# Linear attention with a routed feed-forward part: the order of the results' products, of the loads, and a second bank

## The chip, the cores and the metric

One core of one Trainium2 chip runs the kernel. The time is the device time of one execution in microseconds (us), taken over several runs. TensorE is named PE in the profile (PEld is its loading of weights), VectorE DVE, ScalarE ACT, GpSimd POOL, and SyncE, which issues most of the transfers, SP.

## The reference

The input has 4 batches, 8 heads, 768 steps and 48 values per head. First comes a linear attention with a decay for each key channel, then, for each batch, a feed-forward part for the 128 rows of 768 with the highest score.

```python
for t in range(S):
    kt, vt, rt, wt = (k[:, :, t], v[:, :, t], r[:, :, t], w[:, :, t])
    cur = np.einsum('bhd,bhe->bhde', u[None] * kt, vt)
    y[:, :, t] = np.einsum('bhd,bhde->bhe', rt, state + cur)
    state = wt[:, :, :, None] * state + np.einsum('bhd,bhe->bhde', kt, vt)
# x: y with the heads side by side, 4 x 768 x 384
scores = np.einsum('bsd,d->bs', x, w_gate)
for b in range(B):
    top_idx = np.argpartition(-scores[b], capacity)[:capacity]   # 128 rows
    xe = x[b, top_idx]
    ye = np.maximum(xe @ w1, 0.0) @ w2                           # 384 -> 1024 -> 384
    out[b, top_idx] = xe + sigmoid(scores[b, top_idx])[:, None] * ye
```

## The kernel before, in words

The steps are cut into chunks of 128: 6 chunks for each of 4 batches, 24 in all, with all 8 heads of a chunk worked on at once. Heads lie in pairs: the two heads of a pair take partitions 0 to 63 and 64 to 127 (48 of 64 used), and four pairs lie side by side in the free dimension. Everything is float32; only the ranking uses bfloat16.

For a chunk, `decays_t` (L202) transposes the decays w on TensorE; `scans` (L206) runs two running products over them on VectorE, from the right (L212) and from the left (L224). `scaled` (L239) transposes k and r and multiplies them by these products, which gives K and R (L243). `scores` (L259) multiplies K by R for each head (L264) and `masked` (L269) keeps what lies before the diagonal (`sc`, L273). `outputs_t` (L282) makes the transposed result in one PSUM bank, `ps_yt`: for each pair two products of the values with `sc` (L290, the "value products", over all 128 partitions and half of the columns) and, where the chunk is not the first of its batch, two products of the state carried in with R (L298, the "state products", each on one half of the partitions). `carry_products` (L323) and `carry` (L335) make the state for the next chunk. `rows_out` (L305) transposes the result back into the same bank (`ps_y`), adds the chunk's own-step part `vo` on VectorE (x, L309) and stores it; `row_scores` (L315) makes the rows' routing scores (L318).

The four inputs lie in rings of buffers: 4 each for r, k and w, 5 for v. `load(n)` (L120) issues w, k, r and v of chunk n on SP's queue, each as one transfer of 192 KB in runs of 192 bytes. Chunks 0 to 3 are loaded ahead of the loop, with u and w_gate between them. The two feed-forward matrices of 1.5 MB each come in one issue each (L141).

The order of all work is written out by hand. `turn(i)` (L528) does, in this order: scores, mask, carry and transposed K of chunk i, K of chunk i+1, the rows out of chunk i-1; one piece of the ranking and some pieces of the feed-forward part; R of chunk i+1, the decay transposes of chunk i+2, the results' products and the carry's products of chunk i, further pieces of the feed-forward part; the scans of chunk i+2, the own values of i+1, the row scores of i-1, one more piece of the ranking; and last the loads of chunk i+5. It runs for i from -2 to 24. Every engine keeps to the order in which it is given its instructions, and so does SP with its transfers.

The ranking (`mixture`, L353) of a batch begins two turns after the batch's last chunk and goes piece by piece into later turns: rank transposes (L361), comparisons on VectorE (L380), rank sums (L389), one-hot rows (L405), row numbers (L412, L418), a gather of the 128 rows (L427), their transposes (L436). The feed-forward part (`forward`, L464) follows: 8 hidden products in two groups of four, each group in the one PSUM bank "m" (`ps_h`, L471) and emptied by a ScalarE activation into `hid` (L476), then 8 output products (`ps_f`, L481) in the same bank, and `ye` (L487), which is scattered to the output (L490). For batch 3, and a good part of batch 2, this stands behind the loop. At the end a check of the range of the decays picks a general version, which is not run with these inputs.

Of the kernel before, what the change touches and what calls it, by code (L numbers as in the profile page):

```python
# [10 lines left out]
FP32 = mybir.dt.float32  # L11
# [7 lines left out]
L = 128  # L19
DP = 64  # L20
NBUF = 4
# [17 lines left out]
def kernel(  # L39
# [39 lines left out]
    nc = tc.nc  # L79
    PSUM = bass.MemoryType.PSUM  # L80

    B, H, S, D = r.shape
# [3 lines left out]
    NCH = S // L  # L86
    HP = H // 2
    NDC = C // L
    NFC = F // L
# [27 lines left out]
            if i < len(bufs):  # L117
                nc.any.memset(bufs[i][:, :, D:DP], value)

    def load(n):  # L120
        if n >= N:
            return
        b, ci = chunks[n]
        for bufs, x in ((w_bufs, w), (k_bufs, k), (r_bufs, r), (v_bufs, v)):
            nc.sync.dma_start(
                out=bufs[n % len(bufs)][:, :, 0:D],
                in_=x[b, :, ci * L:(ci + 1) * L, :].rearrange("h t d -> t h d"),
            )

    load(0)  # L130
    u_bc = consts.tile([L, H, D], FP32)
    nc.sync.dma_start(out=u_bc, in_=_rows(u, L))
    load(1)
    wg_bc = consts.tile([L, C], FP32)
    nc.sync.dma_start(out=wg_bc, in_=_rows(moe_w_gate, L))
    load(2)
    load(3)
    w1 = consts.tile([L, NDC, F], FP32)
    w2 = consts.tile([L, NFC, C], FP32)

    def load_weights():  # L141
        nc.sync.dma_start(out=w1, in_=moe_w1.rearrange("(n p) f -> p n f", p=L))
        nc.sync.dma_start(out=w2, in_=moe_w2.rearrange("(n p) c -> p n c", p=L))


    ident = consts.tile([L, L], FP32)
# [135 lines left out]
    def outputs_t(t):  # L282

        n = t["n"]
        vt = v_bufs[n % VBUF]
        old = state.get(n)
        ps = psY.tile([L, HP, L], FP32, tag="y", name="ps_yt")
        for j in range(HP):
            for par in (0, 1):
                nc.tensor.matmul(  # L290
                    ps[DP * par:DP * par + DP, j, :], vt[:, 2 * j + par, :],
                    t["sc"][:, par, j, :], start=True, stop=(old is None),
                )
            if old is None:
                continue
            for par in (0, 1):
                rows = slice(DP * par, DP * par + DP)
                nc.tensor.matmul(  # L298
                    ps[DP * par:DP * par + D, j, :], old[rows, j, :], t["R"][rows, j, :],
                    start=False, stop=True,  # L300
                )
        t["yt"] = lev.tile([L, HP, L], FP32, tag="yt", name="yt")
        nc.scalar.copy(out=t["yt"], in_=ps)  # L303
# [160 lines left out]
    def forward(b, n, rows, where, xe, xeT, gate):  # L464

        hid = mod.tile([L, NFC, L], FP32, name="hid")
        for f0 in range(0, NFC, 4):
            ps = psM.tile([L, 4, L], FP32, tag="m", name="ps_h")
            for q in range(4):
                for dc in range(NDC):  # L470
                    nc.tensor.matmul(  # L471
                        ps[:, q, :], w1[:, dc, (f0 + q) * L:(f0 + q + 1) * L],
                        xeT[:, dc, :], start=(dc == 0), stop=(dc == NDC - 1),
                    )
                if q == 3:
                    nc.scalar.activation(out=hid[:, f0:f0 + 4, :], in_=ps, func=AF.Relu)  # L476
                yield

        ps = psM.tile([L, C], FP32, tag="m", name="ps_f")
        for fc in range(NFC):  # L480
            nc.tensor.matmul(  # L481
                ps, hid[:, fc, :], w2[:, fc, :], start=(fc == 0), stop=(fc == NFC - 1)
            )
            if fc < NFC - 1:
                yield
        ye = mod.tile([L, C], FP32, name="ye", bufs=2)
        nc.vector.scalar_tensor_tensor(  # L487
            out=ye, in0=ps, scalar=gate, in1=xe, op0=ALU.mult, op1=ALU.add
        )
        nc.gpsimd.indirect_dma_start(  # L490
            out=rows, out_offset=where, in_=ye[0:n], in_offset=None,
            bounds_check=(b + 1) * S - 1, oob_is_err=False,
        )
        yield
# [5 lines left out]
    def step(f, n, *more):  # L500
        if 0 <= n < N:
            f(work.setdefault(n, dict(n=n)), *more)
# [25 lines left out]
    def turn(i):  # L528
        if i - 2 >= 0 and i - 2 < N and chunks[i - 2][1] == NCH - 1:
            b = chunks[i - 2][0]  # L530
            mixing.append(mixture(b))
        step(own_products, i + 1)
        step(scores, i)
        step(masked, i)
        step(carry, i - 1, work.get(i))
        step(scaled, i + 1, "K", k_bufs, "right")
        step(back, i)
        step(rows_out, i - 1)
        mix()
        fed(PIECES // 2)  # L540
        step(scaled, i + 1, "R", r_bufs, "left")
        step(decays_t, i + 2)
        step(outputs_t, i)
        step(carry_products, i)
        fed(PIECES - PIECES // 2)
        step(scans, i + 2)
        step(range_check, i + 2)
        step(own_values, i + 1)
        step(row_scores, i - 1)
        mix()  # L550
        load(i + 1 + NBUF)
        if i == 0:
            load_weights()

    with tc.manual_schedule():
        for i in range(-2, N + 1):
# [93 lines left out]
```

## Time and profile before

| | us |
|---|---|
| median of three runs | 272.96 |
| lowest, highest | 271.13, 276.75 |
| the profiled execution | 272.69 |
| its span, from the first to the last record | 270.9 |

The rows in the section below come from this one profiled execution. Times in them count from the start of its span. "x4" behind an operation is a number of records; one float32 product shows as two.

### The profile page before, as it was taken

The numbers are of one execution on the slowest core, as the hardware profiler recorded it, in microseconds if no ns is written. First come the engines' busy times: TensorE is split into PE (matmuls) and PEld (weight loads), VectorE is DVE, ScalarE is ACT, GpSimd is POOL, SyncE is SP. The second block draws the span as 40 slices with busy tenths as digits, with TensorE's granted clock in tenths as the row PEclk, the third lists the DMA queues.
The fourth block names the chain that finished last, engine by engine and source line by source line (L and its number), as shares of the span: only waits on it lengthen the run. The fifth ranks groups of instructions, "written<-read, shape, count | busy, mean of one in ns | idle before, by whom it ended". The sixth has DMA issues, their size and how long they took to land.

```text
span 270.9 us, 5843 instructions
## 1 busy us (share of the span) xinstructions
PE 230.1 (85%) x2290; PEld 169.9 (63%) x2290; DVE 211.8 (78%) x431; ACT 77.0 (28%) x201; POOL 98.9 (37%) x108
## 2 busy tenths in 40 slices
PE   3783999999798699795999899994999899989780
PEld 2572677776665467674688476584778566685740
DVE  6894478999999998999999999789889994373010
ACT  5450203333442121344323213233213301220100
POOL 3243405554433550844055326334236331102000
PEclk9998569999999858999999999999899999999997
DMA  9999999999996363488545635944000000201001
GB/s 129 180 176 166 162 285 327 179 191 205 193 173 115 67 114 87 92 171 119 111 76 109 127 75 96 171 108 72 31 30 2 29 31 23 68 29 29 31 0 42
DMA packets 109732, 29.96 MB, mean 111 GB/s; under 512 B 104576, under 2 KB 108928, under 8 KB 109696
## 3 DMA queue, kind: packets, MB, share of 16 engines
q1 hardware_dynamic: 109184, 27.93, 58.2%
q0 software_dynamic: 512, 1.57, 1.8%
q8 instruction: 20, 0.33, 0.6%
q14 instruction: 16, 0.13, 0.2%
HBM read 23.99 MB, written 5.51 MB: 109 GB/s over the span
## 4 chain that ended last, share of the span: by engine, by line
PE 44%; DVE 7%; ACT 4%; issue 1%; POOL 0%; ACTq 0%
PE ps_h L471 9%; PE ps_f L481 8%; PE ps_yt L290 6%; PE ps_yt L298 6%; PE ps_t L199 5%; PE ps_s L264 4%; PE ps_kv L330 2%; ACT kt L278 1%; ACT hid L476 1%; PE ps_w L199 1%; DVE left L224 1%; PE ps_e L361 1%; DVE right_buf L212 1%; DVE scr L444 1%; PE ps_y L199 1%
## 5 line engine op out<-in xcount | busy, mean ns | idle before, releaser
L255 POOL TENSOR_TENSOR vo<-v_buf,own 128x384 f32<-128x384 f32 x24 | 25.2, 1051 | 106.5 <-DVE own L253 102.4
L290 PE MATMUL ps_yt<-sc,v_buf 128*64 128x128 f32 x384 | 41.8, 309 | 4.0 <-DVE x L309 4.0
L303 ACT COPY yt<-ps_yt 128x512 f32<-128x512 f32 x24 | 14.1, 586 | 106.9 <-PE ps_yt L298 99.0
L273 DVE TENSOR_TENSOR sc<-ps_s,before_f 128x512 f32<-128x512 f32 x48 | 30.8, 682 | 12.4 <-PE ps_s L264 12.4
L298 PE MATMUL ps_yt<-R,state 64*48 64x128 f32 x320 | 35.7, 302 | 0.0
L290 PEld LDWEIGHTS ps_yt<-sc,v_buf 128*64 128x64 f32 x384 | 20.1, 141 | 21.2 <-issue 14.1
L212 DVE TENSOR_TENSOR_SCAN right_buf<-ps_w,from_right 128x511 f32<-128x511 f32 x24 | 29.0, 1210 | 5.3 <-PE ps_w L199 5.3
L248 POOL TENSOR_TENSOR rk<-r_buf,k_buf 128x384 f32<-128x384 f32 x24 | 30.9, 1289 | 4.0 <-DMA r_buf<-in_r_dram 4.0
L224 DVE TENSOR_TENSOR_SCAN left<-ps_w,from_left 128x511 f32<-128x511 f32 x24 | 30.7, 1280 | 0.9
L264 PE MATMUL ps_s<-R,K 48*128 48x128 f32 x384 | 30.6, 304 | 0.0
L264 PEld LDWEIGHTS ps_s<-R,K 48*128 48x128 f32 x384 | 25.7, 204 | 4.6 <-issue 2.3
L471 PE MATMUL ps_h<-xeT,w 128*128 128x128 f32 x192 | 25.5, 283 | 2.0 <-ACT hid L476 1.4
L380 DVE SCALAR_TENSOR_TENSOR ahead<-every,score,behind 128x768 bf16<-128x768 f32 (+5 forms) x24 | 27.0, 1165 | 0.1
L481 PE MATMUL ps_f<-w,hid 128*128 128x384 f32 x64 | 24.3, 506 | 2.2 <-ACT hid L476 2.2
L249 POOL TENSOR_TENSOR rk<-rk,u_bc 128x384 f32<-128x384 f32 x24 | 25.3, 1053 | 2.6 <-DMA u_bc<-in_u_dram 0.8
L199 PE MATMUL ps_w<-ident,w_buf 128*128 128x128 f32 x96 | 16.5, 301 | 10.1 <-DVE slots L162 4.2
L471 PEld LDWEIGHTS ps_h<-xeT,w 128*128 128x128 f32 x192 | 23.1, 195 | 3.0 <-ACT hid L476 1.8
L298 PEld LDWEIGHTS ps_yt<-R,state 64*48 64x48 f32 x320 | 14.0, 123 | 15.2 <-issue 14.8
L278 ACT COPY kt<-ps_t 128x512 f32<-128x512 f32 x24 | 14.0, 585 | 30.3 <-PE ps_t L199 30.1
L199 PE MATMUL ps_t<-ident,r_buf 128*128 128x128 f32 x96 | 16.5, 298 | 3.7 <-ACT kt L278 2.3
L243 DVE TENSOR_TENSOR R<-ps_t,left 128x512 f32<-128x512 f32 x24 | 16.4, 684 | 3.9 <-PE ps_t L199 2.0
L199 PEld LDWEIGHTS ps_w<-ident,w_buf 128*128 128x128 f32 x96 | 12.7, 157 | 10.7 <-issue 10.7
(89 smaller groups left out, 326.1 us busy)
## 6 DMA issues: line engine op xcount, KB each, us to landing
w_buf<-in_w_dram SPq DMA_DIRECT2D x25, 192.0 KB, 4.1
k_buf<-in_k_dram SPq DMA_DIRECT2D x25, 192.0 KB, 4.8
r_buf<-in_r_dram SPq DMA_DIRECT2D x25, 192.0 KB, 5.0
v_buf<-in_v_dram SPq DMA_DIRECT2D x25, 192.0 KB, 4.3
out_dram<-x SPq DMA_DIRECT2D x24, 192.0 KB, 2.1
w<-in_moe_w_dram SPq DMA_DIRECT2D x2, 1536.0 KB, 9.7
u_bc<-in_u_dram SPq DMA_DIRECT2D x1, 192.0 KB, 4.6
wg_bc<-in_moe_w_gate_dram SPq DMA_DIRECT2D x1, 192.0 KB, 5.2
```

Of the source, the lines that this page charges most:

```text
L199: nc.tensor.transpose(ps[:, j, :], src(j), ident)
L212: nc.vector.tensor_tensor_scan(out=flat[:, W - 2::-1], data0=wt[:, W - 1:0:-1], data1=from_right.rearrange("p j t -> p (j t)")[:, W - 2::- ...
L224: nc.vector.tensor_tensor_scan(out=left.rearrange("p j t -> p (j t)")[:, 1:W], data0=wt[:, 0:W - 1], data1=start.rearrange("p j t -> p (j ...
L248: nc.gpsimd.tensor_mul(rk, r_bufs[n % NBUF][:, :, 0:D], k_bufs[n % NBUF][:, :, 0:D])
L249: nc.gpsimd.tensor_mul(rk, rk, u_bc)
L264: nc.tensor.matmul(ps[:, par, j, :], t["K"][rows, j, :], t["R"][rows, j, :], start=True, stop=True,)
L273: nc.vector.tensor_mul(t["sc"][:, par], ps[:, par], _heads(before_f, HP))
L290: nc.tensor.matmul(ps[DP * par:DP * par + DP, j, :], vt[:, 2 * j + par, :], t["sc"][:, par, j, :], start=True, stop=(old is None),)
L298: nc.tensor.matmul(ps[DP * par:DP * par + D, j, :], old[rows, j, :], t["R"][rows, j, :], start=False, stop=True,)
L380: nc.vector.scalar_tensor_tensor(out=ahead[:, c, lo:S], in0=every[:, lo:S], scalar=score[:, b, c:c + 1], in1=behind[:, 0:S - lo], op0=ALU. ...
L471: nc.tensor.matmul(ps[:, q, :], w1[:, dc, (f0 + q) * L:(f0 + q + 1) * L], xeT[:, dc, :], start=(dc == 0), stop=(dc == NDC - 1),)
L481: nc.tensor.matmul(ps, hid[:, fc, :], w2[:, fc, :], start=(fc == 0), stop=(fc == NFC - 1))
```

## The change

It has four parts.

1. Results' products: all eight value products of a chunk are issued first, then all eight state products. The bank's start flag is set by the first pair's value products alone.
2. Loads: the loads of one step are v of chunk n-2, k and r of chunk n-1 and w of chunk n, ahead of the loop and in it; the loop's first turn issues none. The feed-forward matrices are cut into seven pieces (three of 512 KB, four of 384 KB), one issued at the end of each turn from turn 2 on.
3. In the last turn the row scores are made right after the rows out.
4. For the last batch the second group of four hidden products uses the results' bank ("y").

```diff
-    def load(n):
-        if n >= N:
-            return
-        b, ci = chunks[n]
-        for bufs, x in ((w_bufs, w), (k_bufs, k), (r_bufs, r), (v_bufs, v)):
+    def load(bufs, x, n):
+        if n < N:
+            b, ci = chunks[n]
             nc.sync.dma_start(
                 out=bufs[n % len(bufs)][:, :, 0:D],
                 in_=x[b, :, ci * L:(ci + 1) * L, :].rearrange("h t d -> t h d"),
             )
 
-    load(0)
+    def loads(n):
+
+        load(v_bufs, v, n - 2)
+        load(k_bufs, k, n - 1)
+        load(r_bufs, r, n - 1)
+        load(w_bufs, w, n)
+
+    load(w_bufs, w, 0)
+    load(k_bufs, k, 0)
+    load(r_bufs, r, 0)
+    load(w_bufs, w, 1)
     u_bc = consts.tile([L, H, D], FP32)
     nc.sync.dma_start(out=u_bc, in_=_rows(u, L))
-    load(1)
+    loads(2)
+    loads(3)
     wg_bc = consts.tile([L, C], FP32)
     nc.sync.dma_start(out=wg_bc, in_=_rows(moe_w_gate, L))
-    load(2)
-    load(3)
...
-    def load_weights():
-        nc.sync.dma_start(out=w1, in_=moe_w1.rearrange("(n p) f -> p n f", p=L))
-        nc.sync.dma_start(out=w2, in_=moe_w2.rearrange("(n p) c -> p n c", p=L))
+    weights = [
+        (w1[:, i, :], moe_w1[i * L:(i + 1) * L, :]) for i in range(NDC)
+    ] + [
+        (w2[:, i:i + 2, :], moe_w2[i * L:(i + 2) * L, :].rearrange("(n p) c -> p n c", p=L))
+        for i in range(0, NFC, 2)
+    ]
+
+    def load_weights(n):
+        while n > 0 and weights:
+            to, src = weights.pop(0)
+            nc.sync.dma_start(out=to, in_=src)
+            n -= 1
...
         for j in range(HP):
             for par in (0, 1):
                 nc.tensor.matmul(
                     ps[DP * par:DP * par + DP, j, :], vt[:, 2 * j + par, :],
-                    t["sc"][:, par, j, :], start=True, stop=(old is None),
-                )
-            if old is None:
-                continue
+                    t["sc"][:, par, j, :], start=(j == 0), stop=(old is None),
+                    skip_group_check=True,
+                )
+        for j in range(HP if old is not None else 0):
             for par in (0, 1):
                 rows = slice(DP * par, DP * par + DP)
                 nc.tensor.matmul(
                     ps[DP * par:DP * par + D, j, :], old[rows, j, :], t["R"][rows, j, :],
-                    start=False, stop=True,
+                    start=False, stop=True, skip_group_check=True,
                 )
...
-            ps = psM.tile([L, 4, L], FP32, tag="m", name="ps_h")
+
+            pool, tag = (psY, "y") if b == B - 1 and f0 % 8 == 4 else (psM, "m")
+            ps = pool.tile([L, 4, L], FP32, tag=tag, name="ps_h")
...
         step(rows_out, i - 1)
+        if i == N:
+            step(row_scores, i - 1)
         mix()
...
-        step(row_scores, i - 1)
+        if i < N:
+            step(row_scores, i - 1)
         mix()
-        load(i + 1 + NBUF)
-        if i == 0:
-            load_weights()
+        if i > -2:
+            loads(i + 5)
+        if i > 1:
+            load_weights(1 if NCH > 2 else 100)
```

## Rows read from the trace of the kernel before

**Rows 1.** The page: busy time of each engine, and VectorE's slices.

```profile
PE 230.1 (85%) x2290; PEld 169.9 (63%) x2290; DVE 211.8 (78%) x431; ACT 77.0 (28%) x201; POOL 98.9 (37%) x108
...
DVE  6894478999999998999999999789889994373010
```

**Rows 2.** Stretches: length, busy PE, PEld, DVE, ACT, POOL, granted clock, DMA share, GB/s.

```profile
17.66:32.26 14.60, 10.21 (x88) 6.47 (x85) 9.01 (x18) 3.25 (x10) 5.04 (x6) 0.74 1.26 165
32.26:42.06 9.80, 9.80 (x86) 7.71 (x84) 6.54 (x12) 2.15 (x6) 1.29 (x2) 0.69 1.15 280
42.06:63.58 21.52, 20.80 (x240) 14.84 (x236) 19.73 (x39) 7.25 (x21) 10.55 (x12) 1.00 1.11 221
98.97:108.64 9.67, 9.58 (x108) 7.53 (x106) 8.25 (x17) 2.16 (x7) 1.93 (x3) 0.79 0.40 88
205.68:216.15 10.47, 9.42 (x99) 6.85 (x98) 10.37 (x20) 2.63 (x7) 5.26 (x5) 1.00 0.05 19
```

**Rows 3.** Waits of VectorE for TensorE: us in total, times, longest.

```profile
DVE sc L273 <- PE ps_s L264: 12.4, 10, 4.1
...
DVE R L243 <- PE ps_t L199: 2.0, 5, 0.7
```

**Rows 4.** Transfers: GB/s in 40 slices; issues of w with KB and us to landing.

```profile
GB/s 129 180 176 166 162 285 327 179 191 205 193 173 115 67 114 87 92 171 119 111 76 109 127 75 96 171 108 72 31 30 2 29 31 23 68 29 29 31 0 42
...
w_buf<-in_w_dram SPq DMA_DIRECT2D x25, 192.0 KB, 4.1
```

**Rows 5.** SP's issues in order of time (start, us): both loads of chunk 3's w.

```profile
14.72 1.09 SPq L125 DMA_DIRECT2D w_buf<-in_w_dram  x1
...
20.15 1.38 SPq L125 DMA_DIRECT2D w_buf<-in_w_dram  x1
```

**Rows 6.** TensorE in order of time, 20 to 26 us.

```profile
20.52 0.66 PE L199 MATMUL ps_t<-ident,r_buf 128*128 128x128 f32 x4 [0.24 <-ACT kt L278]
25.34 1.09 PE L199 MATMUL ps_w<-ident,w_buf 128*128 128x128 f32 x4 [4.15 <-DMA w_buf<-in_w_dram]
```

**Rows 7.** The chain (start, us to the next), and TensorE in order of time.

```profile
114.05 0.37 PE ps_yt L290 x4
114.42 0.35 PE ps_yt L298 x4
...
116.94 1.09 PE ps_s L264 x16
```

```profile
67.47 1.09 PE L290 MATMUL ps_yt<-sc,v_buf 128*64 128x128 f32 x16
68.39 0.62 PE L330 MATMUL ps_kv<-v_buf,kt 128*64 128x48 f32 x16
```

**Rows 8.** VectorE in order of time: score masks of chunks 2, 5, 6 and 23.

```profile
34.39 1.29 DVE L273 TENSOR_TENSOR sc<-ps_s,before_f 128x512 f32<-128x512 f32 x2 [4.07 <-PE ps_s L264]
...
58.02 1.29 DVE L273 TENSOR_TENSOR sc<-ps_s,before_f 128x512 f32<-128x512 f32 x2 [0.39 <-PE ps_s L264]
...
64.92 1.28 DVE L273 TENSOR_TENSOR sc<-ps_s,before_f 128x512 f32<-128x512 f32 x2
...
226.98 1.29 DVE L273 TENSOR_TENSOR sc<-ps_s,before_f 128x512 f32<-128x512 f32 x2 [2.96 <-PE ps_s L264]
```

**Rows 9.** Behind the loop, in order of time: VectorE's ye, TensorE's waits.

```profile
234.94 0.62 DVE L487 SCALAR_TENSOR_TENSOR ye<-ps_f,gate,xe 128x384 f32<-128x384 f32 x1 [0.36 <-PE ps_f L481]
...
236.09 0.32 PE L361 MATMUL ps_e<-ident,score 128*128 128x128 f32 x1 [0.64 <-DVE score L318]
...
253.69 2.94 PE L471 MATMUL ps_h<-xeT,w 128*128 128x128 f32 x24 [0.75 <-ACT hid L476]
257.32 0.91 PE L481 MATMUL ps_f<-w,hid 128*128 128x384 f32 x2 [0.69 <-ACT hid L476]
```

**Rows 10.** TensorE in order of time at 93 us.

```profile
93.07 0.69 PE L290 MATMUL ps_yt<-sc,v_buf 128*64 128x128 f32 x4 [2.23 <-DVE x L309]
93.69 0.67 PE L298 MATMUL ps_yt<-R,state 64*48 64x128 f32 x4
```

## The prediction

> **What bounds the kernel now.** I read the busy line and the slices of the page first. TensorE shows 85% and VectorE 78% of the span, and VectorE's slices are at 9 for most of the loop [rows 1]: two engines share the bound, so time taken from one is worth only what the other leaves idle. The stretches cut at the start of each turn's score products say which of the two it is. The turn 205.68 to 216.15 holds 10.37 us of VectorE work in 10.47 us: VectorE sets it. The two turns from 17.66 to 42.06 hold 9.01 of 14.60 and 6.54 of 9.80, with a granted clock of 0.74 and 0.69: there VectorE starves, by 5.59 + 3.26 us. In the next three turns, 42.06 to 63.58, it idles 21.52 - 19.73 = 1.79 us [rows 2]. The waits say for whom: ten times for the score products, 12.4 us together, five times for the product behind R, 2.0 us [rows 3].
>
> Why does the second turn starve? Chunk 3's w is issued at 14.72 and again at 20.15, because the preload has chunks 0 to 3 and the first turn asks for chunk 3 once more; the list of transfers has 25 w loads for 24 chunks [rows 4, 5]. TensorE's transpose of that w waits for the second copy until 25.34, 4.15 us. After that gap the engine runs at its lower level, 1.2 GHz of 2.4, as the four transposes show that take 1.09 us there [rows 6], and the next scores reach VectorE 4.07 us late [rows 8].
>
> **Part 1, loads.** A load is 196,608 bytes; the slices from 7 to 34 us move 162 to 180 GB/s, 170 or so: 1.16 us per load [rows 4]. The second w of chunk 3 is the 19th in the queue and there at 25.34, so the nth is there near 3.3 + 1.16 n us. In the new order (w, k, r, w, u, then v, k, r, w twice) chunk 3's w is the 13th and is not repeated: 18.4 us. It is needed when the r transposes before it end, which start at 20.52 [rows 6]: near 21. Turn 2 needs k, r and w of the next chunk, 16th to 18th: 21.9 to 24.2, needed a turn of about 7 us later than in turn 1, near 26 to 28. Turn 3 needs the 20th to 22nd: 26.5 to 28.8, needed near 33. So no wait for a transfer is left, with 2.6 us to spare or more. The other bound is SP's issue spacing: from 14.72 to 20.15 it takes 5.43 us for four, 1.36 each [rows 5]. By it, and 4.1 us from issue to landing [rows 4], the 13th is there at 12 x 1.36 + 4.1 = 20.4 and the 18th at 27.2: just in time. I take 1.16, which comes from the bytes moved.
>
> With the 4.15 us gap gone the clock need not fall, and VectorE is late by nothing: from 58.02 to 64.92 one turn of its work takes 6.90 us [rows 8]. The idle time from 17.66 to 63.58 is 5.59 + 3.26 + 1.79 = 10.6 us. I take 10.2 of it; the last three turns need part 2 for theirs (about 1.2 us). The rest stays as the small steps between products and VectorE. The lower bound is 5: the wait goes, but the half clock comes anyway, from the wait for x that TensorE then has in the same place.
>
> The feed-forward weights, 3.1 MB in two issues at the end of turn 0, become seven pieces of 0.5 and 0.4 MB, issued after turns 2 to 8. Their first use is in batch 0's feed-forward part, four turns after the last piece. In these turns the queue carries four loads, one output row block (5 x 1.16 = 5.8 us) and a piece; at the 285 to 327 GB/s of the slices in which the weights went by [rows 4] a piece adds 1.2 to 1.8 us. That is 7.0 to 7.6 us against turns of 7 to 8: the transfers about keep up, and each load has one to two turns of lead. On SP each load still stands behind the output block of its turn, as before. Cost taken: 0, bounds 0 to 2 us.
>
> **Part 2, results' products in two runs.** In the chain of waits a pair of value products takes 0.37 us between starts and a pair of state products 0.35, alternating four times: 4 x 0.72 = 2.88 us. Eight value products alone, at a batch's first chunk, take 68.39 - 67.47 = 0.92 us, or 0.23 a pair; the score products, in the state products' form of half-height tiles, take 1.09 for eight including one change of form [rows 7]. So each change of form costs about 0.13 us, and there are eight. New: 0.92 + 1.09 + 0.14 = 2.15, a saving of 0.72 us in each of 20 turns, 14.5 us of TensorE time. Bounds: 0, if the changes are not what costs, to 1.0 in a turn at half clock.
>
> How much of it counts? In turns that VectorE sets, nothing. In the others it shortens the waits above. Of the 12.4 us, four waits before 60 us (first 4.07, last 0.39) are 5.5 and already in part 1; the last, at 226.98, is 2.96 [rows 3, 8]; five in the middle make 3.9. TensorE is late through several turns in a row there, so savings add up until VectorE is the late one. I take 3.6 of the 3.9 and 0.7 of the 2.0 us behind R: 4.3. At the loop's end two turns' savings are 1.44, of which I let 1.2 through, since the second of them also waits for VectorE's x to free the bank; the last turn's own products give 0.72 more: 1.9.
>
> **Part 3, row scores ahead.** In the last turn the row score stands behind ye, which waits for TensorE from 234.58 to 234.94 and takes 0.62; TensorE's sixth rank transpose waits 0.64 us for that score [rows 9]. Moved into the idle time, the score ends 0.9 us sooner and the wait goes; ye then starts some 0.15 us later, and with it the bank for the next hidden products comes free: 0.64 - 0.15 = 0.5 us. Bounds: 0, if the bank is what ends last, to 0.9.
>
> **Part 4, second bank for the last batch.** TensorE waits 0.75 us before the second four hidden products and 0.69 before the output products [rows 9]. With the second group in the other bank the first wait goes whole; the output products' bank is free earlier, and their first four chunks need only the first half of the hidden values, so four of them (1.4 us) hide the second activation: 1.4 together. If the tile is waited for whole, 0.7.
>
> **Sum.** 10.2 + 4.3 + 1.9 + 0.5 + 1.4 = 18.3. Against it: VectorE becomes the bound in more turns, so TensorE idles longer. At 93.07 it came back from 2.23 us of idleness into half clock: 0.62 us from the value pair to the state pair, where the chain has 0.37 [rows 7, 10]; the following turn had VectorE idle for 9.67 - 8.25 = 1.42 us at a mean clock of 0.79 [rows 2]. I allow one more such fall: 1.4 us. Net 16.9. The profiled execution took 272.69 us (span 270.9); the median of the runs is 272.96, near enough to use the same figure: 272.7 - 16.9 = 255.8.
>
> The Trainium skill bears on this ("TensorE: Matmul & The Clock Gate", Part 1: The HAM clock gate): the throttled state is the default and activity releases it, so a TensorE made idler can be clocked down. The trace agrees at 93.07. By this rule alone the change would pay its savings back in some turns; that is the second rival.
>
> **Rivals.**
> (a) The start gains only half: loads arrive late or the clock falls there anyway (5 instead of 10.2): 261. For it: the queue is full from the start [rows 4]. Against: the 13th load has 2.6 us to spare.
> (b) The clock falls in four more turns that VectorE sets, at 1.4 [rows 2] to 4.1 us (the wait at 34.39 [rows 8]) each: 3 more than allowed at about 2.4 us, 263. For it: idle times of TensorE grow by 0.72 in just these turns. Against: where TensorE has feed-forward products to do, it stays busy.
> (c) The two runs save nothing, because something else than the change of form costs 0.13 us: parts 2 and the 1.2 in part 1 go, 7.4 us: 263. Against: the 0.92 us row.
> (d) Slower than before: the pieces and loads of turns 2 to 8 don't keep up, and each of these seven turns waits for its transfers. To eat the 16.9 us it must be 2.4 us a turn, so a turn's transfers must take over 9.4 us where I count 7.0 to 7.6: 275 at 9.7. Against it: before, the same queue moved more in the same stretch without a wait of that size.
>
> **How the numbers follow.** Forecast 0.62, own range 252 to 259.5; (a) 0.13; (b) 0.12; (c) 0.09; (d) 0.02; the rest, 0.02, is a gain too small for any of these reasons. The range of 250.5 to 263 takes in (a) and most of (b) and (c), and below, a start with no idle time and no added fall (254.4) with all middle waits gone. A measurement of this kernel tells about 2%, or 5.5 us, from no change. Faster by more: 0.95; within: 0.03 (the rest and a little of (b)); slower: 0.02.
>
> **What would show it.** 24 loads of each input; no wait of the w transposes for a transfer near 21 us; full clock from 16 to 60 us; VectorE's third score mask at about 27 instead of 34.39 and the one of 64.92 at about 55; value and state products each in one run, some 2.1 us together; the five middle waits for scores down to a fraction; no wait between the last batch's two hidden groups. Wrong, if the turns before 60 us last over 7.5 us, if the clock sinks in several turns where it was whole, or if the products' stretch still takes 2.9 us.

## The result, and the profile after

| | before | change |
|---|---|---|
| median of this comparison, us | 274.60 (4 runs, 271.13 to 276.75) | 253.86 (4 runs, 253.60 to 256.09) |
| ratio to before, 95% interval | | 0.935 [0.9245, 0.9454] |
| the profiled execution, us | 272.69 | 253.60 |
| its span, us | 270.9 | 251.8 |

The change is faster by 6.5%; the forecast was 255.8. The ratios here and below leave out, on both sides, runs in a slower state with a lower granted clock, so they are not the quotients of the medians. What follows goes by the profiled executions, as the prediction's sum did: 272.69 - 253.60 = 19.1 us to explain, where the prediction had 16.9. The interval of the ratio, 14.9 to 20.6 us of 272.7, takes in both.

The page first: busy times, and the slices of VectorE and of the granted clock.

```profile
PE 210.3 (84%) x2290; PEld 172.9 (69%) x2290; DVE 211.1 (84%) x431; ACT 77.0 (31%) x201; POOL 98.9 (39%) x108
...
DVE  6999999999999999997999999888999995472010
...
PEclk9999999999979789997999999998999999999995
```

VectorE has the same work (211.1 against 211.8 us [rows 1]) and its slices are at 9 from the second on, where before they showed 8, 9, 4, 4, 7 and 8 there. TensorE has 20 us less busy time with the same 2290 matrix products.

The start, on TensorE in order of time (start, us, line, operation; in brackets the idle time before it and what ended it):

```profile
19.43 0.66 PE L216 MATMUL ps_t<-ident,r_buf 128*128 128x128 f32 x4 [0.24 <-ACT kt L295]
19.93 0.60 PE L216 MATMUL ps_w<-ident,w_buf 128*128 128x128 f32 x4
21.39 1.09 PE L308 MATMUL ps_yt<-sc,v_buf 128*64 128x128 f32 x16 [0.87 <-DVE x L327]
22.42 1.08 PE L316 MATMUL ps_yt<-R,state 64*48 64x128 f32 x16
23.42 0.67 PE L348 MATMUL ps_kv<-v_buf,kt 128*64 128x48 f32 x16
```

The transposes of chunk 3's w stand where they waited 4.15 us [rows 6], with no wait and at full clock. The value products are one run of 22.42 - 21.39 = 1.03 us, the state products one of 1.00: 2.03 us where the alternating ones took 2.88. TensorE now waits for VectorE's x (0.87), not the other way round.

The transfers: issues of w (KB, median us to landing), and SP's issue of chunk 3's w, the 13th.

```profile
w_buf<-in_w_dram SPq DMA_DIRECT2D x24, 192.0 KB, 4.7
```

```profile
12.57 1.14 SPq L123 DMA_DIRECT2D w_buf<-in_w_dram  x1
```

There are 24 loads instead of 25, and the w that was issued at 14.72 and a second time at 20.15 [rows 5] is issued once, at 12.57.

VectorE in order of time: the score masks of chunks 2, 6 and 23, which answer to [rows 8].

```profile
25.63 1.28 DVE L290 TENSOR_TENSOR sc<-ps_s,before_f 128x512 f32<-128x512 f32 x2
...
53.22 1.28 DVE L290 TENSOR_TENSOR sc<-ps_s,before_f 128x512 f32<-128x512 f32 x2
...
210.60 1.29 DVE L290 TENSOR_TENSOR sc<-ps_s,before_f 128x512 f32<-128x512 f32 x2 [2.10 <-PE ps_s L281]
```

From 25.63 to 53.22 are four turns of 6.90 us each, the length of a turn that VectorE sets. The waits by line (us in total, times, longest) say the same of the whole kernel:

```profile
PE ps_yt L308 <- DVE x L327: 8.6, 11, 1.7
...
DVE sc L290 <- PE ps_s L281: 2.9, 3, 2.1
...
DVE R L260 <- PE ps_t L216: 1.8, 2, 1.2
```

VectorE's waits for scores fell from 12.4 us in ten waits to 2.9 in three [rows 3]; TensorE's waits for VectorE's x come eleven times.

Behind the loop, TensorE in order of time, the places of [rows 9]:

```profile
217.77 0.82 PE L379 MATMUL ps_e<-ident,score 128*128 128x128 f32 x6
218.64 2.94 PE L491 MATMUL ps_h<-xeT,w 128*128 128x128 f32 x24
...
232.46 5.62 PE L491 MATMUL ps_h<-xeT,w 128*128 128x128 f32 x48 [0.57 <-ACT xeT L456]
237.92 5.33 PE L501 MATMUL ps_f<-w,hid 128*128 128x384 f32 x16
```

The six rank transposes are one piece without the 0.64 us wait. The 48 records of batch 3's hidden products are one piece too: they wait for ScalarE's xeT once, before the first (0.57 us, as they did before), and neither their second half nor the output products wait for ScalarE's `hid` any more.

A ledger by VectorE's score masks (the start of each, us, from VectorE's rows in order of time) tells where the 19.1 us are. Each column is one execution. The last three columns belong to the experiments.

| mask of chunk | before | change | gain so far | loads only | two runs only | no repeat |
|---|---|---|---|---|---|---|
| 0 | 13.92 | 12.72 | 1.20 | 12.76 | 13.89 | 14.00 |
| 1 | 19.82 | 18.73 | 1.09 | 20.27 | 21.05 | 20.86 |
| 2 | 34.39 | 25.63 | 8.76 | 27.64 | 31.63 | 28.23 |
| 6 | 64.92 | 53.22 | 11.70 | 56.66 | 59.80 | 57.26 |
| 10 | 101.10 | 88.84 | 12.26 | 92.86 | 95.43 | 92.92 |
| 11 | 110.77 | 97.69 | 13.08 | 102.51 | 104.28 | 105.04 |
| 13 | 128.42 | 115.31 | 13.11 | 120.16 | 121.90 | 123.33 |
| 14 | 137.48 | 125.05 | 12.43 | 130.65 | 131.55 | 132.39 |
| 18 | 176.21 | 161.73 | 14.48 | 169.38 | 168.23 | 171.12 |
| 22 | 217.80 | 202.50 | 15.30 | 212.13 | 208.98 | 212.73 |
| 23 | 226.98 | 210.60 | 16.38 | 221.30 | 217.09 | 221.90 |

After the masks come VectorE's last x (234.02 before, 216.79 after: 17.23), the first hidden products of batch 2 (236.25 and 218.64: 17.61), those of batch 3 (249.99 and 232.46: 17.53), the output products of batch 3 (257.32 and 237.92: 19.40). The end of the span keeps 19.1 of it.

One turn loses: from mask 13 to 14 the gain shrinks by 0.68 us. TensorE there, and VectorE:

```profile
114.89 0.54 PE L379 MATMUL ps_e<-ident,score 128*128 128x128 f32 x3 [2.82 <-ACT kt L295]
116.00 0.90 PE L379 MATMUL ps_e<-ident,score 128*128 128x128 f32 x3 [0.57 <-ACT every L382]
116.69 1.49 PE L491 MATMUL ps_h<-xeT,w 128*128 128x128 f32 x6
117.97 1.06 PE L216 MATMUL ps_t<-ident,r_buf 128*128 128x128 f32 x4
```

```profile
119.07 0.69 DVE L260 TENSOR_TENSOR R<-ps_t,left 128x512 f32<-128x512 f32 x1 [1.16 <-PE ps_t L216]
```

After two waits of TensorE (2.82 us before the first group of rank transposes and 0.57 before the second) the clock fell: the r transposes take 1.06 us instead of 0.66, and R waits 1.16 us for them. The granted clock of 110 to 126 us is 0.89.

### The profile page after: what moved, and what is told of

Read it like the earlier page. It is cut to its first block, busy times and chain, and to the rows that moved or that the text cites. A ratio compares the mean times of both kernels' runs of the same rounds, so it can differ in the third digit from the quotient of the medians.

```text
span 251.8 us, 5841 instructions
## 1 busy us (share of the span) xinstructions
PE 210.3 (84%) x2290; PEld 172.9 (69%) x2290; DVE 211.1 (84%) x431; ACT 77.0 (31%) x201; POOL 98.9 (39%) x108
## 4 chain that ended last, share of the span: by engine, by line
PE 33%; DVE 16%; issue 3%; ACT 2%; POOL 0%
PE ps_h L491 9%; PE ps_f L501 7%; PE ps_t L216 4%; PE ps_yt L308 3%; PE ps_s L281 3%; PE ps_yt L316 3%; DVE ahead L398 2%; DVE sc L290 2%; DVE left L241 2%; DVE right_buf L229 2%; PE ps_kv L348 1%; PE ps_w L216 1%; DVE K L260 1%; DVE R L260 1%; PE ps_e L379 1%
## 5 line engine op out<-in xcount | busy, mean ns | idle before, releaser
L308 PE MATMUL ps_yt<-sc,v_buf 128*64 128x128 f32 x384 | 28.8, 296 | 8.6 <-DVE x L327 8.6
L308 PEld LDWEIGHTS ps_yt<-sc,v_buf 128*64 128x64 f32 x384 | 22.5, 147 | 13.9 <-DVE x L327 11.6
L281 PE MATMUL ps_s<-R,K 48*128 48x128 f32 x384 | 28.8, 291 | 0.0
L281 PEld LDWEIGHTS ps_s<-R,K 48*128 48x128 f32 x384 | 24.1, 193 | 4.7 <-issue 1.6
L316 PE MATMUL ps_yt<-R,state 64*48 64x128 f32 x320 | 23.8, 293 | 0.0
L316 PEld LDWEIGHTS ps_yt<-R,state 64*48 64x48 f32 x320 | 18.4, 130 | 4.0 <-issue 3.9
L216 PEld LDWEIGHTS ps_t<-ident,r_buf 128*128 128x128 f32 x96 | 11.6, 151 | 11.3 <-DVE K L260 5.6
```

Source lines behind the costliest of these rows:

```text
L216: nc.tensor.transpose(ps[:, j, :], src(j), ident)
L281: nc.tensor.matmul(ps[:, par, j, :], t["K"][rows, j, :], t["R"][rows, j, :], start=True, stop=True,)
L308: nc.tensor.matmul(ps[DP * par:DP * par + DP, j, :], vt[:, 2 * j + par, :], t["sc"][:, par, j, :], start=(j == 0), stop=(old is None), ski ...
L316: nc.tensor.matmul(ps[DP * par:DP * par + D, j, :], old[rows, j, :], t["R"][rows, j, :], start=False, stop=True, skip_group_check=True,)
```

## The experiments

### One part at a time

The first four kernels take the kernel before and add one thing each. Measured beside them, the kernel before took 269.77 to 276.48 us. The runs of one kernel spread by 3 us and more, so a column of the ledger tells where time went in one execution, and the intervals of the ratios tell how sure the sum is.

**No repeat.** The first turn's repeated loads of chunk 3 are left out, nothing else.

```diff
-        load(i + 1 + NBUF)
+        if i > -2:
+            load(i + 1 + NBUF)
```

> The kernel before, with one edit: the loop's first turn no longer loads chunk 3 a second time. Theory (the start was lost to the repeat): chunk 3's w is then the 15th load, there near 3.3 + 15 x 1.16 = 20.7 us, just when the r transposes before it end, so the 4.15 us wait goes to under 0.5, the clock stays at full level, the mask of chunk 6 comes at 55 to 57 instead of 64.92, and the time falls by 7.5 to 9.5 us, to about 264. Rival (the order of use is what counts): the wait only shortens to 2 to 3 us, the clock still falls, and the gain is under 4 us.

Measured: 267.82 us (265.47 to 268.87), 0.985 [0.964, 1.005]; profiled 267.56. TensorE in order of time, chunk 3's w transposes, and the place where it went wrong:

```profile
23.01 0.60 PE L199 MATMUL ps_w<-ident,w_buf 128*128 128x128 f32 x4
...
95.11 1.12 PE L199 MATMUL ps_t<-ident,r_buf 128*128 128x128 f32 x4 [1.89 <-DVE K L243]
...
102.92 2.08 PE L264 MATMUL ps_s<-R,K 48*128 48x128 f32 x16
```

and VectorE's mask behind them:

```profile
105.04 1.29 DVE L273 TENSOR_TENSOR sc<-ps_s,before_f 128x512 f32<-128x512 f32 x2 [2.56 <-PE ps_s L264]
```

The wait for w is gone, and masks 1 to 6 take 57.26 - 20.86 = 36.40 us instead of 45.10, which is 8.7 us less. Mask 1 came 1.04 us later than before, though, and a later mask 1 shortens the wait for a transfer that lands when it does: by mask 6 the kernel is 64.92 - 57.26 = 7.7 us ahead. In the fourth kernel below, which has the start of the kernel before, mask 6 came at 63.94, 6.7 us behind this one. So not loading chunk 3 twice is worth about 7 us, most of the start. Then, in turn 10, the clock fell after a wait of 1.89 us, the scores took 2.08 us instead of 1.16, and VectorE waited 2.56 us for them: masks 6 to 22 take 155.47 us where before they took 152.88. So the start's gain reached the end only in part. The expected time was missed, and by the ratio alone the kernel can't be told from the one before.

**Loads only.** The new order of the loads and the weights in pieces, without the two runs, the row scores and the second bank.

```diff
...
-        load(i + 1 + NBUF)
-        if i == 0:
-            load_weights()
+        if i > -2:
+            loads(i + 5)
+        if i > 1:
+            load_weights(1 if NCH > 2 else 100)
```

> The changed kernel's loads (order, lead, no repeat, weights in pieces) alone, all else as before. Theory: the start gains what the changed kernel showed at the mask of chunk 6 (64.92 - 53.22 = 11.7) less the three waits for scores that the two runs removed there (about 1.2): 10 to 10.8 us, nothing behind it, so about 262. Rival (the two runs were needed at the start as well): 7 us or less.

Measured: 266.57 us (264.62 to 267.34), 0.979 [0.962, 0.996]; profiled 267.34. Mask 0 is at 12.76, as in the change (12.72) and 1.2 us earlier than in the kernels with the old order: this step, which the prediction had not counted, belongs to the loads. Masks 1 to 6 take 36.39 us, as without the repeat, and by mask 6 the gain is 64.92 - 56.66 = 8.3 us. The 1.9 us from 36.39 to the change's 34.49 are what the alternating products keep: masks 2 to 5 show a wait of 0.39 us each, as the last one did before [rows 8]. In the middle 2.6 us were lost again (155.47 us from mask 6 to 22), this time by clock falls in turns 13 and 19. The expected 262 was missed by that loss, and because mask 6 gained 8.3 us where 10 or more were expected.

**Two runs only.** All value products first, then all state products; the old loads.

```diff
...
-                    t["sc"][:, par, j, :], start=True, stop=(old is None),
-                )
-            if old is None:
-                continue
+                    t["sc"][:, par, j, :], start=(j == 0), stop=(old is None),
+                    skip_group_check=True,
+                )
+        for j in range(HP if old is not None else 0):
...
```

> The kernel before with the value and state products in two runs, all else as before. Theory (VectorE takes back what it does not wait for): of 20 x 0.85 = 17 us of TensorE time only the waits for scores come back: about 1 in the half-clock turn, 1.5 in the three turns after it, 3.6 in the middle, 1.9 at the loop's end, 8 us together, so about 264.5 (262 to 267). Rival 1 (TensorE is the bound all through): 14 us or more. Rival 2 (the clock falls take it back): under 4 us.

Measured: 264.89 us (262.34 to 266.73), 0.9775 [0.9575, 0.9976], as expected; profiled 262.34, the fastest of its runs. The w transposes still wait for the second copy:

```profile
25.68 0.63 PE L199 MATMUL ps_w<-ident,w_buf 128*128 128x128 f32 x4 [2.33 <-DMA w_buf<-in_w_dram]
```

Masks 6 to 22 take 208.98 - 59.80 = 149.18 us, as in the change (149.28) and 3.7 less than before. The middle and the loop's end thus belong to the two runs alone. By mask 6 it is 5.1 us ahead where about 2.5 were expected: the wait for the second copy is 2.33 us instead of 4.15, with mask 1 1.2 us later than before.

**Row scores and bank only.**

```diff
+            pool, tag = (psY, "y") if b == B - 1 and f0 % 8 == 4 else (psM, "m")
+            ps = pool.tile([L, 4, L], FP32, tag=tag, name="ps_h")
...
+        if i == N:
+            step(row_scores, i - 1)
...
```

> The kernel before with the row scores ahead in the last turn and the second bank for the last batch, all else as before. Theory: 0.4 from the scores and 1.9 from the bank (a wait costs TensorE a restart of about 0.2 besides its shown 0.7): 2.3 us, about 270.4. Rival: only the shown waits, 0.75 + 0.69, or 0.7 if the hidden values are waited for whole: 0.7 to 1.4 us in all.

Measured: 269.66 us (nine runs from 268.25 to 272.90, and one of 315.37), 0.9933 [0.9872, 0.9994]; profiled 269.51. From mask 23 (226.03) to the end of the span (267.7) are 41.67 us; before it was 270.9 - 226.98 = 43.92. The 2.25 us are what the change gains there too (0.38 and 1.87). TensorE in order of time, batch 3:

```profile
248.68 5.62 PE L472 MATMUL ps_h<-xeT,w 128*128 128x128 f32 x48 [0.57 <-ACT xeT L438]
254.14 5.33 PE L482 MATMUL ps_f<-w,hid 128*128 128x384 f32 x16
```

From the start of the hidden products to the start of the output products it took 257.32 - 249.99 = 7.33 us before and 254.14 - 248.68 = 5.46 here.

### What costs in the alternating products

**Staggered.** The change with the state products of pair j issued one pair later, so that six of the eight changes of form are back, but no state product follows directly on the value product of its own pair.

```diff
...
+        value(0)
+        for j in range(1, HP):
+            value(j)
+            if old is not None:
+                carried(j - 1)
+        if old is not None:
+            carried(HP - 1)
```

> The changed kernel with the results' products staggered: value pairs 0 and 1, state 0, value 2, state 1, value 3, states 2 and 3. No state pair follows at once the value pair of its own columns, but the form changes five times inside instead of once. Theory (each change of form costs TensorE about 0.14 us, from (2.88 - 2.03) / 6): the stretch takes 2.03 + 4 x 0.14 = 2.6 us. Rival (a state product waits for the value product that it adds to): no such pair follows directly any more, so 2.0 to 2.1 us.

Measured: 259.67 us in one run. TensorE in order of time:

```profile
22.45 0.66 PE L308 MATMUL ps_yt<-sc,v_buf 128*64 128x128 f32 x8
23.03 0.42 PE L317 MATMUL ps_yt<-R,state 64*48 64x128 f32 x4
23.39 0.44 PE L308 MATMUL ps_yt<-sc,v_buf 128*64 128x128 f32 x4
23.76 0.42 PE L317 MATMUL ps_yt<-R,state 64*48 64x128 f32 x4
24.11 0.44 PE L308 MATMUL ps_yt<-sc,v_buf 128*64 128x128 f32 x4
24.48 0.64 PE L317 MATMUL ps_yt<-R,state 64*48 64x128 f32 x8
25.05 0.67 PE L357 MATMUL ps_kv<-v_buf,kt 128*64 128x48 f32 x16
```

The stretch takes 25.05 - 22.45 = 2.60 us. Alternating, with eight changes counted into the next operation, it was 2.88; in two runs, with two, 2.03. With six it should be 2.03 + 4 x 0.14 = 2.59. So it is in 17 of the 20 turns (2.60 or 2.61), as 17 of 20 show 2.88 or 2.89 before and 16 of 20 show 2.03 or 2.04 in the change; the turns left over take longer, wholly or partly at half clock. The price goes by the number of changes of form and not by what depends on what: 0.85 / 6 = 0.14 us each at full clock.

### The weights in pieces

**Weights whole.** The change, with the feed-forward matrices in two issues at the end of turn 0 as before.

```diff
...
-        if i > 1:
-            load_weights(1 if NCH > 2 else 100)
+        if i == 0:
+            load_weights()
```

> The changed kernel with the feed-forward weights in two whole issues at the end of turn 0, as before. Theory (the start is safe by the order and the missing repeat, the pieces do little): 3.1 MB stand ahead of the loads of turn 1 on, about 9 us at 330 GB/s, against loads that are needed one to two turns (7 to 14 us) after issue; so a wait of 0 to 3 us in turns 2 to 4, and a time of 254 to 257. Rival (the pieces are what freed the start): turns 2 to 4 wait 5 us or more, the clock falls, 259 or more.

Measured: 255.01 us (253.60 to 255.46), 0.939 [0.932, 0.945]. TensorE in order of time shows the only place where the 3 MB delay loads:

```profile
39.35 0.66 PE L206 MATMUL ps_t<-ident,k_buf 128*128 128x128 f32 x4 [0.42 <-DMA k_buf<-in_k_dram]
...
41.52 0.63 PE L206 MATMUL ps_t<-ident,r_buf 128*128 128x128 f32 x4 [0.64 <-DMA r_buf<-in_r_dram]
```

Mask 5 is 0.62 us later than in the change (46.94 against 46.32) and mask 6 by 0.63. The theory holds: the time is in its range, and by these waits the pieces are worth 0.6 us. The profiled executions of the two kernels took the same 253.60 us, and the two medians, 1.2 us apart, don't tell 0.6 from nothing.

### What the half clock costs

**Filler.** The change with transposes of the identity, which nobody reads, put where TensorE idles: before or after the r and w transposes of turns 8 to 10, and before the rank transposes of turns 13 and 19.

```diff
+    def fill(count):
+        ps = psM.tile([L, 4, L], FP32, tag="m", name="ps_z")
+        for q in range(count):
+            nc.tensor.transpose(ps[:, q % 4, :], ident, ident)
...
+        if i in (NCH + 2, NCH + 3):
+            fill(12)
```

> The changed kernel with transposes of the identity into the free hidden-product bank where TensorE idles: 12 before the results' products of turns 8 and 9, 14 before the R transposes of turn 10, 20 before the rank transposes of turns 13 and 19. Theory: the clock stays at full level from 65 to 125 us and around 175; in turns 8 to 10 that is worth nothing, since VectorE has no gap there, and in turns 13 and 19 it takes away the waits of 1.16 and about 0.7 us for the product behind R: 1 to 2 us faster than the changed kernel. Rival (those waits come from the late transposed K and not from the clock): no gain, or a loss of up to 1 us from the added work. Rival 2 (half clock costs in turns 8 to 10 too): 3 us or more.

Measured: 258.32 us (255.91 to 259.75), 0.950 [0.944, 0.957]. From 64 to 110 us the granted clock is now whole; the stretch in the change had 0.89. The columns are the length, busy PE, PEld, DVE, ACT, POOL, the granted clock, DMA share and GB/s, the filler first:

```profile
64.00:110.00 46.00, 38.41 (x508) 32.92 (x506) 44.71 (x84) 14.13 (x39) 21.08 (x20) 1.00 0.77 149
```

```profile
64.00:110.00 46.00, 38.66 (x469) 32.73 (x467) 44.70 (x84) 13.98 (x38) 21.11 (x20) 0.89 0.76 147
```

VectorE is busy 44.7 us in both, and masks 8 to 13 take 46.27 us against 46.29. So the half clock of turns 8 to 10 costs the change nothing. The change's own runs say it without an edit: in the profiled execution TensorE's products at 71.67 ran at half clock,

```profile
71.67 1.98 PE L308 MATMUL ps_yt<-sc,v_buf 128*64 128x128 f32 x16 [1.69 <-DVE x L327]
73.58 1.76 PE L316 MATMUL ps_yt<-R,state 64*48 64x128 f32 x16
```

and in the repeat of the change reported below the same products ran at full clock:

```profile
71.55 1.09 PE L308 MATMUL ps_yt<-sc,v_buf 128*64 128x128 f32 x16 [1.69 <-DVE x L327]
```

Masks 8 and 9 are 9.68 us apart in both. In turns 13 and 19 the filler did harm, more than the theory or a rival had. The second rank transposes wait 2.08 us for VectorE's K, where they had waited 0.57 for ScalarE,

```profile
117.39 0.54 PE L379 MATMUL ps_e<-ident,score 128*128 128x128 f32 x3 [2.08 <-DVE K L260]
```

and these turns take 11.15 and 11.20 us instead of 9.74 and 9.69. I take it that the extra tile moved the rank transposes to another bank; the trace shows the wait, not that cause. What the clock costs in turn 13 had to be asked in another way.

### The exponential ahead of the rank transposes

In turn 13 ScalarE gets the exponential of the gate (line 470), which waits 2.65 us for VectorE, ahead of the copy of the transposed K (`kt`), for which TensorE then waits 2.82 us. ScalarE in the change:

```profile
114.16 0.20 ACT L470 ACTIVATE neg<-neg 128x1 f32<-128x1 f32 x1 [2.65 <-DVE neg L467]
```

Two kernels move the exponential and the four small VectorE operations that hang on it.

**Exponential later**: issued in the next turn, behind `kt`.

```diff
         step(back, i)
+        for power, finish in late:
+            power()
         step(rows_out, i - 1)
...
+        while late:
+            late.pop(0)[1]()
```

> The changed kernel with the gate's exponential issued after the next turn's copy of the transposed K on ScalarE, and the rest of the gate on VectorE at the end of that turn (batches 0 and 1). Theory: in turns 13 and 19 TensorE's 2.8 us idle time is the copy waiting behind the exponential, which waits for VectorE; with the exponential behind the copy TensorE idles under 1.5 us there, the clock holds, the waits behind R (1.16 and about 0.7) and the 0.27 us waits for the exponential go: 1.5 to 2.3 us faster than the changed kernel, near 252. Rival (VectorE is the bound there with or without them): within 0.5 us of the changed kernel.

Measured: 253.81 us (252.28 to 254.40), 0.933 [0.928, 0.939]. The first group of rank transposes starts at 113.00 after a wait of 0.24, but the second waits for the copy of the first, now behind the exponential on ScalarE:

```profile
115.48 0.54 PE L379 MATMUL ps_e<-ident,score 128*128 128x128 f32 x3 [1.94 <-ACT every L382]
```

The r transposes behind it take 1.12 us, at half clock, and masks 12 to 14 take 19.63 us against 20.04, masks 18 to 20 20.16 against 20.71. The median is that of the change, as the rival had it, but the reason is another: the wait only moved, and the next kernel shows that what it causes did cost.

**Exponential last**: issued behind the copies of the ranks (`every`) in the next turn.

```diff
...
         mix()
+        for power, finish in late:
+            power()
         fed(PIECES // 2)
...
```

> The change, with the gate's exponential issued after the copies of the ranks (every) of the next turn, and what hangs on it at that turn's end. Theory: in turn 13 the second ps_e waits behind the exponential on ScalarE (0.57 shown in the change's trace), TensorE's clock falls at 116 us, and R then waits 1.16 us for transposes at half clock; with the exponential out of the way the wait of ps_e goes, the clock stays and masks 12 to 14 and 18 to 20 take together up to 1 us less than the 40.75 us of the change: 252 to 253 us. Rival: the second ps_e waits for something next in line just as long, the clock falls anyway, and the time is within 0.5 us of the change's.

Measured: 252.03 us (251.18 to 254.26), 0.932 [0.926, 0.937], beside 254.25 for the change, run again with it. TensorE in order of time, and VectorE's R:

```profile
112.26 0.54 PE L379 MATMUL ps_e<-ident,score 128*128 128x128 f32 x3 [0.24 <-ACT kt L295]
113.37 0.54 PE L379 MATMUL ps_e<-ident,score 128*128 128x128 f32 x3 [0.57 <-ACT every L382]
113.75 0.83 PE L501 MATMUL ps_h<-xeT,w 128*128 128x128 f32 x6
116.20 0.66 PE L216 MATMUL ps_t<-ident,r_buf 128*128 128x128 f32 x4 [1.61 <-DVE K L260]
```

```profile
116.96 0.69 DVE L260 TENSOR_TENSOR R<-ps_t,left 128x512 f32<-128x512 f32 x1 [0.35 <-PE ps_t L216]
```

The rank transposes wait 0.24 and 0.57 us, the r transposes run at full clock, and R waits 0.35 instead of 1.16. The granted clock of 110 to 126 us is 1.00 where the change has 0.89. Masks 12 to 14 take 18.98 us (20.04 in the change), masks 18 to 20 19.69 (20.71). That is 2.1 us, more than the 1 us expected as a bound. In turn 13, 0.81 us come from R's wait and 0.27 from one that the expectation had left out, VectorE's own wait for the exponential; in turn 19 it is 0.46 from the waits of R and of the scan behind it, 0.27, and 0.21 from the scores of chunk 20. The theory holds in what it says of R and of the clock, but not in the wait that it named: the second ps_e still waits 0.57 us, and what went is the first one, 2.82 us to 0.24. The kernel moves TensorE's work ahead and keeps the clock up at once, so the two are not told apart. By its median this version is the fastest of the study, 2.2 us below the change measured beside it. The intervals of the two ratios overlap, but of its six runs five lie below all six of the change.

### The clock at the start

In the profiled executions of before and of the four kernels with one part each, mask 1 lies between 19.82 and 21.22 us, and the trace shows why: the clock rose at 15.16 in that of before, and in the four others, with mask 1 past 20 us, products ran at half clock until past 17 us. (The expectation below calls these runs of the kernel before; they are other kernels, three of them with its start.) Can more work of TensorE make it rise sooner?

**Warm start.** The change with products of the identity into a bank that is free: six before the loop, three in turn -1.

```diff
+        if i == -1:
+            warm(3)
...
+        warm(6)
```

> The change, with six more products of the identity (into a bank that is free then) before the loop and three more in turn -1, whose results nobody reads. Theory: the runs of the kernel before differ by when TensorE's clock first rises (15.2 us in the profiled one, later in three others), so more work of TensorE at the start makes it rise earlier: masks 0 and 1 are 0.5 to 2 us earlier than 12.72 and 18.73, and the runs spread less. Rival: the start is set by the loads and the clock rises when it did; the added products then delay the first transposes by up to 0.5 us and the time is that of the change or up to 0.5 us more.

Measured: 254.15 us (253.18 to 255.58), 0.939 [0.9355, 0.9425]. TensorE's first score products, here,

```profile
9.54 1.16 PE L281 MATMUL ps_s<-R,K 48*128 48x128 f32 x16 [0.50 <-DVE R L260]
```

and in the change, run again beside it (line 281 again, then the first transposes at full clock):

```profile
9.42 2.08 PE L281 MATMUL ps_s<-R,K 48*128 48x128 f32 x16
...
13.96 0.66 PE L216 MATMUL ps_t<-ident,r_buf 128*128 128x128 f32 x4 [0.68 <-ACT kt L295]
```

The clock is up at least 4.4 us earlier, so the edit does what it was to do. But mask 0 is at 12.71 (12.72), since VectorE's scans set it, and mask 1 at 18.39 instead of 18.62. The time is that of the change, and its runs spread by 2.4 us where the change's spread by 3.0. The theory's price falls: a rise at 13.96 instead of before 9.54 costs the change 0.2 to 0.3 us. A rise past 17 us costs more: in the staggered kernel and in that with the loads only, which have the change's loads, mask 1 came at 19.77 and 20.27, 1.0 and 1.5 us later than in the change. No profile of the change shows such a rise. What makes its runs spread stays open.

**Both edits.**

> Both edits: the later exponential and the added products at the start. If both theories hold, the sum of the two, 251 to 252.5 us; if both rivals hold, 253.6 to 254.5.

Measured: 252.34 us (251.96 to 253.64), 0.932 [0.928, 0.935]. That is in the range given for both theories, but it is the gain of the later exponential, and nothing on top. Its profiled execution (253.33) lost some at the start, on TensorE and on VectorE:

```profile
22.78 1.94 PE L316 MATMUL ps_yt<-R,state 64*48 64x128 f32 x16
```

```profile
26.46 0.69 DVE L290 TENSOR_TENSOR sc<-ps_s,before_f 128x512 f32<-128x512 f32 x1 [1.11 <-PE ps_s L281]
```

The clock fell at about 21 us, and in a turn of 6.9 us, unlike in those of 9.7, that cost VectorE 1.11 us.

**The change again.**

> The change itself, beside the three others on the same chip: 253.6 to 256, the spread of its own runs, with the clock's first rise between 14 and 16 us.

Measured: 254.25 us (253.21 to 256.23), 0.940 [0.935, 0.946], the clock rising at 13.96.

## Why the prediction was right

| term of the sum | predicted | by the trace |
|---|---|---|
| start | 10.2 | 11.7 by mask 6 |
| waits of the middle | 4.3 | 4.3: 3.6 from mask 6 to 22, with the 0.7 lost in turn 13 added |
| loop's end | 1.9 | 17.23 - 15.30 = 1.9 |
| row scores ahead | 0.5 | 17.61 - 17.23 = 0.4 |
| second bank | 1.4 | 1.9 |
| one more clock fall | -1.4 | -0.7 |
| sum | 16.9 | 19.5; 19.1 at the end of the span |

**The start** was right in its reason: "With the 4.15 us gap gone the clock need not fall, and VectorE is late by nothing". The experiment without the repeat shows that the second load of chunk 3 alone is worth about 7 us (6.7 and 7.7 by mask 6, against two executions with the old start); the two runs add 36.39 - 34.49 = 1.9, where I had put 1.2. The size is short because the sum began at 17.66 us: the first mask is 1.2 us earlier already, by the order of the loads, and counted from mask 1 the gain is 11.70 - 1.09 = 10.6, the whole idle time of [rows 2]. The third mask came at 25.63 (I had said 27) and that of chunk 6 at 53.22 (55).

**Weights in pieces**: cost 0 was right; whether they save 0.6 us against the old way under the new order is not told from nothing. GpSimd's `vo` is shown waiting for them twice (6.8 us together), and no wait of VectorE for `vo` is shown.

**Two runs**: a change of form costs 0.14 us (0.13 predicted), which the staggered order shows to be the cause. The saving is 0.85 us in a turn and not 0.72, because the state products in one run, with the change behind them, take 1.00 us and not the 1.09 of the score products.

The Trainium skill says of this ("TensorEngine Tiling (Array Packing)", Key Properties) that a change of tiling mode drains TensorE. The trace agrees in that each change costs time, 0.14 us here; no row shows the drain itself.

**Middle and clock.** The term of 4.3 was met in sum, not in its parts: the waits for scores in the middle fell from 3.9 us to 0.75 (0.54 and 0.21), but those behind R only from 2.0 to 1.8, since turn 13 put 1.16 there. "I allow one more such fall: 1.4 us" was not met: the clock sank in several turns where it was whole (the products' stretch at 71.67, 81.36 and 92.06, then turns 13 and 19), as rival (b) has it, so one of the signs of being wrong came up. The first three cost nothing. Turn 13 lost 0.7 us against before; against a kernel without the falls in turns 13 and 19 (the exponential last) the change loses about 1.5 us there, the 2.1 us less the two waits of 0.27 for the exponential. A fall costs by what is left of the products' stretch: in two runs at half clock it took 75.27 - 71.67 = 3.60 us in the change, alternating it took 4.88 before (from the value products at 93.07 [rows 10] to the carry's products, which start at 97.95). Where VectorE sets a turn of 9.7 us there is room for the first. The two kernels with the start mended and the products still alternating lost 2.6 us each to such falls, and so they look worth less than their start.

**Second bank.** "The first wait goes whole", with 0.75 us, was the mis-sized term. A wait shown as 0.7 us moves the next start by more: the 24 records take 2.94 us and the next ones start 3.70 and 3.63 us after them, of which the products without a wait need 5.46 / 2 = 2.73. Each wait cost 0.93 us on average.

**Rivals.** (a) and (c) are refuted by the ledger and the staggered order; (b) holds in its mechanism and not in its price; (d) would have shown as long turns from chunk 2 on, and those to chunk 6 take 6.90 us.

The sum is short by about 2 us, and the errors don't cancel: all but 0.1 go the same way. The largest is the 1.2 us of the first mask, which I had not counted.

## What to carry to other kernels

A transfer that is asked for twice costs little in bytes and much in place: here TensorE waited for the second copy, and the gap cost 4 us of waiting and then the clock. Count the loads of each input in the list of transfers against the number of tiles. Put matrix products of one form together, price what alternates by the number of changes, and ask of every wait on an in-order engine (here ScalarE's exponential) what harmless work stands behind it.

## What the runs showed of the hardware

A change of form between products of full and half height costs TensorE 0.14 us at full clock, in the two orders tried (2.88 and 2.60 us against 2.03). The clock first rises at different times in kernels with the same work at the start (13.96 us in the change, past 17 us in the staggered kernel), and with nine products of the identity added at the start it rose before 9.54 us. A half clock costs nothing in one turn (masks 8 to 13: 46.27 and 46.29 us) and more than 1 us in a shorter one (1.11 us at 26.46), by the slack that VectorE leaves TensorE in it. A wait shown before a product understates what it costs: 0.75 and 0.69 us were shown where 0.93 on average were gained.
